# Folding the width axis twice on VectorE, width transforms in groups of 160, and small TensorE tiles placed side by side

## The chip, the core and the metric

One core of one Trainium2 chip runs the whole program. The metric is device time of one execution in microseconds (us); the number for a kernel is the median of its runs. Engines are named as in the profile: PE is TensorE (PEld its weight loads), DVE is VectorE, ACT is ScalarE, POOL is GpSimd, SP issues the DMAs.

## What is computed

```python
def reference(A_x, A_w_r, A_w_i, B_x, B_w1, B_b1, B_w2, B_b2):
    # A: y = irfft2(rfft2(x over rows S=2048 and width D=640) * (w_r + 1j*w_i))
    # B: h = gelu_tanh(x @ w1 + b1), 640 -> 1536; y = h @ w2 + b2, 1536 -> 640
    x = A_x                                    # (1, 2048, 640), bf16
    xn = _layernorm(x, axis=-1)
    return x + _A_ref(xn, A_w_r, A_w_i) + _B_ref(xn, B_w1, B_b1, B_w2, B_b2)
```

## The kernel before

The 2048 rows are held as 16 chunks `c` of 128 partitions. Every transform is a product with a constant table that is loaded from HBM. The program is a list of operations with priorities and guessed durations; a planner (`Sched`) fixes, when the program is built, the order on each engine, which of ACT or DVE makes a copy, and which of the eight PSUM slots a result takes. Each engine then runs its list strictly in order and waits on semaphores. The stages:

- **Ring stage** (per chunk): DVE makes the layernorm statistics of two chunks at a time (L528 to L534; the power -1/2 is on POOL, L532, `rstd`), normalizes (L547), and folds the width once (L562): the sum and the difference of the row and its mirror image, 320 columns each. PE transposes the normalized chunk (L554, five matmuls with `ident`) for the dense branch, and multiplies the folded chunk by `gtab` (five matmuls of 128 columns), a first step of the row transform. DVE or ACT copies both from PSUM (`xnT`, `XW`).
- **First dense layer**: 48 groups of five matmuls of 512 columns (`xnT`, `W`), each followed by one gelu on ACT (`gT`, L583) that adds the bias column `b1col`. The planner gives these groups to PE where it has nothing more urgent. The bias column is made by a small matmul and a DVE copy (L512, L514), both with priority 50 while the ring has about 100.
- **Spectral stage** (eight pairs of 128-row groups `q`): six matmuls of 320 columns with `etab` per group (the width transform), a copy (`Xb`), four of 322 with `mtab`, a copy (`Y`), two DVE multiplications by the filter (`T`, L622) and five DVE additions (`Z`, L632, L636) per pair, ten matmuls of 128 with `ntab`, a copy (`XV`).
- **Final stage** (per chunk): six matmuls of 320 with `getab` (the inverse width transform), a copy (`Wf`), then 24 matmuls of 320 of the second dense layer (`gT`, `XW` which by then holds W2) and four of 320 with `htab` into the same PSUM. Two of the four exist only because the width is still folded. POOL adds x and the bias b2 beforehand (L688, `b2bc`), DVE adds that to PSUM (`ost`, L704), and a DMA writes the chunk. Groups of the first dense layer that are left over stand between.

Nearly all matmuls are recorded under one helper line, L450, all copies under L457 (ACT) and L458 (DVE), so groups are told apart by the names of their tiles. SP issues the loads in the order written: x, `ident`, W1, `gtab`, `etab`, `mtab`, 24 pieces of the filter, `ntab`, `getab`, `htab`, `b2bc`, W2.

Of the kernel before, what the change touches and what calls it, by code (L numbers as in the profile page):

```python
# [288 lines left out]
def _tables():  # L289
    pi = np.pi  # L290
    T = {}
    s1 = np.arange(128)
    G = np.zeros((128, 16, 128))
    H = np.zeros((128, 16, 128))
    for s2 in range(16):
        for q in range(16):
            for i in range(4):
                m1 = 16 * i + q
                ang = 2 * pi * ((m1 * (16 * s1 + s2)) % 2048) / 2048
                G[:, s2, q * 8 + i] = np.cos(ang)  # L300
                G[:, s2, q * 8 + 4 + i] = -np.sin(ang) if m1 else np.cos(pi * s1)
                H[q * 8 + i, s2] = np.cos(ang)
                H[q * 8 + 4 + i, s2] = np.sin(ang) if m1 else np.cos(pi * s1)
    T["G"], T["H"] = G, np.stack([H, -H], axis=2)
    th = 2 * pi * ((np.arange(321)[:, None] * (2 * np.arange(320)[None, :] + 1)) % 1280) / 1280
    ck = np.where((np.arange(321) == 0) | (np.arange(321) == 320), 1.0, 2.0)[:, None] / (S * D)
    Ec, Es = np.cos(th)[:320].T, -np.sin(th)[1:].T
    GEc, GEs = (ck * np.cos(th))[:320], (-ck * np.sin(th))[1:]

    def five(a, b):  # L310
        z = np.zeros((64, 320))
        return np.concatenate([a[0:128], a[128:256], np.concatenate([a[256:320], z]), np.concatenate([z, b[0:64]]),
                               b[64:192], b[192:320]], axis=1)
    T["E"] = five(Ec, Es)

    T["GE"] = five(GEc, np.concatenate([GEs[256:320], GEs[0:256]]))
    M = np.zeros((2, 4, 128, 128))
    N = np.zeros((2, 2, 128, 128))
    for sp in range(2):
        for i in range(4):  # L320
            for m2 in range(16):
                p = 16 * i + m2
                s2 = np.arange(16)
                r, u = s2 * 8 + i, s2 * 8 + 4 + i
                a1 = 2 * pi * ((m2 * s2) % 16) / 16
                c, s = np.cos(a1), np.sin(a1)
                rr, ir, ri, ii = M[sp]
                NA, NB = N[sp]
                if sp and i == 0:
                    pq = 64 + m2  # L330
                    a2 = 2 * pi * ((s2 * (2 * m2 + 1)) % 32) / 32
                    c2, t2 = np.cos(a2), np.sin(a2)
                    rr[r, p], ri[r, p], ir[r, p], ii[r, p] = c, s, -s, c
                    rr[u, pq], ri[u, pq], ir[u, pq], ii[u, pq] = c2, t2, -t2, c2
                    NA[p, r], NB[p, r], NA[pq, u], NB[pq, u] = c, s, c2, t2
                    continue
                pq = 64 + 16 * ((4 if sp else 3) - i) + 15 - m2
                rr[r, p], rr[u, p], ir[r, p], ir[u, p] = c, s, -s, c
                ri[r, p], ri[u, p], ii[r, p], ii[u, p] = s, -c, c, s
                rr[r, pq], rr[u, pq], ir[r, pq], ir[u, pq] = c, s, s, -c  # L340
                ri[r, pq], ri[u, pq], ii[r, pq], ii[u, pq] = -s, c, c, s
                NA[p, r], NA[pq, r], NB[p, r], NB[pq, r] = c, c, s, -s
                NA[p, u], NA[pq, u], NB[p, u], NB[pq, u] = -s, -s, c, -c
    T["M"] = M.transpose(2, 0, 1, 3)
    T["N"] = np.stack([N[:, 0], N[:, 1], -N[:, 1]], axis=1).transpose(2, 0, 1, 3)
    T["I"] = np.eye(128)
    return T
# [392 lines left out]
```

## Time and profile before

| | |
|---|---|
| median of 3 runs | 197.65 us (197.29 to 197.73) |
| profiled execution, its own time | 198.18 us |
| its span, first to last instruction | 196.4 us |
| PE busy | 172.5 us (88%), 1265 matmuls |
| DVE, ACT, POOL busy | 88.3, 75.1, 28.3 us |
| mean granted TensorE clock | 0.974 of full speed |
| DMA | 17.84 MB |

Busy times are sums over the whole span; PE's includes stretches at the lower clock. A matmul's recorded duration includes the time that it takes to leave the array, so that the records of neighbours overlap: the pace of a run of matmuls is read from the start of one group to the start of the next.

### The profile page before, as it was taken

To read this page: it belongs to the slowest core of one execution; us is meant where nothing else is said; L and a number is where in the kernel's file an instruction comes from. 1 tells how busy PE (TensorE), PEld (TensorE's weight loads), DVE (VectorE), ACT (ScalarE), POOL (GpSimd) and SP (SyncE) were. 2 spreads that over 40 slices of the span, in tenths; PEclk is the share of its full clock that TensorE was granted. 3 is DMA by queue.
4 is the path that set the end of the run, shared out by engine and by line. 5 is a ranking of instruction groups with operands and counts; after the bars stand their busy time and mean duration, and the time that the engine had idled before them with its cause. 6 is when DMAs were issued, how large, how long until landed. Compare 5 with 4: busy or idle time off the path is not lost.

```text
span 196.4 us, 3073 instructions
## 1 busy us (share of the span) xinstructions
PE 172.5 (88%) x1265; PEld 113.7 (58%) x1265; DVE 88.3 (45%) x221; ACT 75.1 (38%) x110; POOL 28.3 (14%) x32
## 2 busy tenths in 40 slices
PE   0149760899999999999999999999999999999993
PEld 0135420566567777875677777775457775436772
DVE  0999899869619899967111111111001111001211
ACT  2004500845477679885711111114651113660100
POOL 1111112200000000000823222222002222000200
PEclk9999996589999999999999999999999999999999
DMA  6999999990000000039422222222000201000111
GB/s 179 378 394 301 120 120 132 139 355 13 3 0 0 3 3 0 3 76 376 135 82 71 69 67 68 77 80 79 0 3 33 67 33 37 0 0 0 37 54 48
DMA packets 14374, 17.84 MB, mean 91 GB/s; under 512 B 1304, under 2 KB 13208, under 8 KB 14232
## 3 DMA queue, kind: packets, MB, share of 16 engines
q1 hardware_dynamic: 14360, 17.65, 35.8%
q8 instruction: 10, 0.16, 0.4%
q14 instruction: 4, 0.03, 0.1%
HBM read 15.02 MB, written 2.62 MB: 90 GB/s over the span
## 4 chain that ended last, share of the span: by engine, by line
PE 85%; DVE 11%; DMA 2%; ACT 0%; issue 0%
PE ps L450 82%; DVE stats L528 5%; PE ps L554 4%; DMA XV<-in_A_x_dram 2%; DVE T L547 1%; DVE T L562 1%; DVE mv L530 1%; DVE xnT L458 1%; DVE ost L704 0%; DVE XW L458 0%; ACT gT L583 0%; DVE nmr L534 0%; DVE ve L531 0%; DVE b1col L514 0%
## 5 line engine op out<-in xcount | busy, mean ns | idle before, releaser
L450 PE MATMUL ps<-xnT,W 128*128 128x512 bf16 x240 | 56.9, 388 | 0.0
L450 PE MATMUL ps<-XW,gT 128*128 128x320 bf16 x384 | 54.8, 299 | 0.8 <-ACT gT L583 0.8
L704 DVE TENSOR_TENSOR ost<-ps,Wf 128x640 bf16<-128x640 f32 x16 | 13.2, 824 | 87.0 <-PE ps L450 87.0
L450 PEld LDWEIGHTS ps<-XW,gT 128*128 128x128 bf16 x384 | 37.5, 98 | 15.9 <-ACT gT L583 1.5
L583 ACT ACTIVATE gT<-ps,b1col 128x512 bf16<-128x512 f32 x48 | 32.3, 689 | 30.6 <-PE ps L450 20.1
L688 POOL TENSOR_TENSOR Wf<-Wf,b2bc 128x640 f32<-128x640 bf16 x16 | 22.2, 1394 | 125.1 <-DVE ost L704 67.1
L450 PEld LDWEIGHTS ps<-xnT,W 128*128 128x128 bf16 x240 | 23.5, 100 | 25.1 <-issue 1.7
L457 ACT ACTIVATE Wf<-ps 128x640 bf16<-128x640 f32 x16 | 11.2, 703 | 52.2 <-PE ps L450 51.9
L554 PE MATMUL ps<-ident,T 128*128 128x128 bf16 x80 | 8.8, 277 | 12.5 <-DVE b1col L514 7.2
L528 DVE BATCH_NORM_STATS2 stats<-XV 128x6 f32<-128x320 bf16 x32 | 13.7, 467 | 4.9 <-DMA XV<-in_A_x_dram 4.9
L450 PE MATMUL ps<-getab,XV 128*128 128x320 bf16 x96 | 15.3, 299 | 0.0
L554 PEld LDWEIGHTS ps<-ident,T 128*128 128x128 bf16 x80 | 6.8, 126 | 14.7 <-DVE b1col L514 7.7
L450 PE MATMUL ps<-etab,XW 128*128 128x320 bf16 x96 | 14.7, 299 | 0.0
L622 DVE TENSOR_TENSOR T<-Y,Wf 128x1288 bf16<-128x1288 bf16 x16 | 12.5, 823 | 0.6 <-ACT Y L457 0.5
L457 ACT ACTIVATE Xb<-ps 128x640 bf16<-128x640 f32 x15 | 10.6, 706 | 3.3 <-PE ps L450 2.5
L450 PEld LDWEIGHTS ps<-etab,XW 128*128 128x128 bf16 x96 | 9.4, 97 | 3.9
L450 PEld LDWEIGHTS ps<-getab,XV 128*128 128x128 bf16 x96 | 9.4, 98 | 3.8 <-ACT XV L457 0.2
L450 PE MATMUL ps<-Wf,htab 128*128 128x320 bf16 x64 | 11.3, 299 | 0.0
L457 ACT ACTIVATE XW<-ps 128x640 bf16<-128x640 f32 x6 | 4.1, 700 | 17.9 <-PE ps L450 17.9
L450 PE MATMUL ps<-Xb,mtab 128*128 128x322 bf16 x64 | 10.4, 300 | 0.0
L450 PE MATMUL ps<-ntab,Z 128*128 128x128 bf16 x160 | 10.2, 219 | 0.0
L450 PEld LDWEIGHTS ps<-ntab,Z 128*128 128x128 bf16 x160 | 9.6, 98 | 0.9
(33 smaller groups left out, 107.7 us busy)
## 6 DMA issues: line engine op xcount, KB each, us to landing
XV<-in_A_x_dram SPq DMA_DIRECT2D x4, 640.0 KB, 8.0
Wf<-in_A_x_dram SPq DMA_DIRECT2D x16, 160.0 KB, 2.2
out_dram<-ost SPq DMA_DIRECT2D x16, 160.0 KB, 1.8
W<-in_B_w_dram SPq DMA_DIRECT2D x3, 640.0 KB, 7.7
XW<-in_B_w_dram SPq DMA_DIRECT2D x1, 1920.0 KB, 8.0
htab<-c_H SPq DMA_DIRECT2D x1, 1024.0 KB, 11.5
Wf<-in_A_w_r_dram SPq DMA_DIRECT2D x4, 160.5 KB, 13.5
Wf<-in_A_w_i_dram SPq DMA_DIRECT2D x4, 160.5 KB, 12.3
```

Source lines behind the costliest of these rows:

```text
L450: ins = e.matmul(o_, lhsT=lw, rhs=rh, start=st, stop=sp_)
L457: return e.activation(dst(), src(), ACT.Copy)
L458: return e.tensor_copy(dst(), src())
L528: K.op([("dve", 0.4)], pr, lambda e, _, c=c, h=h: e.bn_stats(stats[:, c, 6 * h:6 * h + 6], view(XV, c * D + H2 * h, [[1, H2]])), reads=[B_ ...
L530: K.op([("dve", 0.12)], pr, lambda e, _, c=c: e.bn_aggr(mv[:, c, :], stats[:, c, :]), reads=[B_st[c - a]], writes=[B_mv])
L547: norm_ops.append(K.op([("dve", 0.32)], pr, lambda e, _, c=c, xnv=xnv: e.tensor_scalar(out=xnv(0, [[1, D]]), in0=view(XV, c * D, [[1, D]]) ...
L554: ins = e.transpose(ps(tps.slot, 0, 512).bitcast(BF)[:, 128 * j:128 * j + 128], xnv(128 * j, [[1, 128]]), ident[:])
L562: K.op([("dve", dve_us(H2, 2))], pr - 0.2, lambda e, _, k=k, op=op, xnv=xnv, xfv=xfv: e.tensor_tensor(out=xfv(H2 * k, [[1, H2]]), in0=xnv( ...
L583: K.op([("act", act_us(512, 1))], pr + 50, lambda e, _, q4=q4, fc=fc, hps=hps: e.activation(gT[:, fc, 512 * q4:512 * q4 + 512], ps(hps.slo ...
L622: filt_ops.append(K.op([("dve", dve_us(4 * KP, 2))], pr, lambda e, _, k=k, Y=Y, TB=TB, pair=pair: e.tensor_tensor(out=view(TT, TB.slot * 8 ...
L688: K.op([("pool", pool_us(640))], 50, lambda e, _, xr=xr, xo=xo: e.tensor_tensor(out=xov(xo), in0=view(Wf, XR + xr.slot * D, [[1, D]]), in1 ...
L704: K.op([("dve", dve_us(640))], 95, lambda e, _, xo=xo, os_=os_, fps=fps: e.tensor_tensor(out=ost[:, os_.slot, :].rearrange("p (h n) -> p h ...
```

## The change

The row is folded a second time: after the first fold DVE adds and subtracts the two halves of each 320 columns again, which leaves four groups of 160. The width transform and its inverse then work in groups of 160 on a table of 800 columns (`etab`, `getab`) in place of 1920. As 160 is 128 and 32, each product has a full part and a rest of 32; the four rests are stored together as a fifth block of 128, and a helper, `five`, issues them as matmuls that use 32 of the array's rows. Where the rests are on the output side (`gtab`, `ntab`), four matmuls with 32 weight columns write to partitions 0, 32, 64 and 96 of one PSUM bank. The products with `mtab` become eight matmuls of 64 rows by 64 columns of weights, four to a position of the array. On the way out DVE unfolds two chunks at once: two operations from 160 to 320, two from 320 to 640, so that only two matmuls with `htab` per chunk are left, and `htab` has half its columns.

Beside that: the bias column's priority is 200; `Z` is made in two operations per pair in place of five; x and its sum with b2 have buffers of their own (`xr`, `xo`), so that their loads wait for nothing; every wait of an engine for an earlier operation of its own (but on PE) is now a semaphore wait; and the durations by which the planner decides are other numbers.

```diff
@@ durations for the planner @@
 def mm_us(n):
-    return max(n / 2400.0 + 0.003, 0.061)
+    return max(n / 2400.0 + 0.003, 0.0265)
...
-LAT = {"pe": 0.25, "dve": 0.12, "act": 0.15, "pool": 0.15}
+LAT = {"pe": 0.2, "dve": 0.12, "act": 0.15, "pool": 0.1}
@@ Sched.sync @@
                     if o.eng == "pe":
                         continue
-                    raw = any(d in b.writers for b in o.reads)
-                    if not raw:
-                        continue
                 need.append(d)
@@ tables @@
-        etab = sb("etab", [128, 1920])
-        mtab = sb("mtab", [128, 8, 128])
+        etab = sb("etab", [128, 800])
+        mtab = sb("mtab", [128, 2, 2, 2, 64])
-        getab = sb("getab", [128, 1920])
-        htab = sb("htab", [128, 32, 128])
+        getab = sb("getab", [128, 800])
+        htab = sb("htab", [128, 16, 128])
@@ bias column @@
-        K.op([("pe", 0.1)], 50, lambda e, _: e.matmul(ps(B_b1ps.slot, 0, NFC), ...
+        K.op([("pe", 0.1)], 200, lambda e, _: e.matmul(ps(B_b1ps.slot, 0, NFC), ...
-        K.op([("dve", 0.2)], 50, lambda e, _: e.tensor_copy(b1col[:], ...
+        K.op([("dve", 0.08)], 200, lambda e, _: e.tensor_copy(b1col[:], ...
@@ second fold, product with gtab @@
+            for k, op in enumerate((ALU.add, ALU.subtract)):
+                K.op([("dve", dve_us(H2, 2))], pr - 0.2, lambda e, _, k=k, op=op, x1v=x1v, xfv=xfv: e.tensor_tensor(
+                    out=xfv(Q4 * k, [[H2, 2], [1, Q4]]), in0=x1v(0, [[H2, 2], [1, Q4]]), in1=x1v(H2 - 1, [[H2, 2], [-1, Q4]]), op=op),
+                    reads=[x1], writes=[xf])
-                (ps(aps.slot + j // 4, 128 * (j % 4), 128 * (j % 4) + 128), xfv(128 * j, [[1, 128]]), gtab[:, c, :], True, True) for j in range(5)]),
+                (ps(aps.slot, 128 * g, 128 * g + 128), xfv(Q4 * g, [[1, 128]]), gtab[:, c, :], True, True) for g in range(4)] + [
+                (ps(aps.slot + 1, 0, 128)[32 * g:32 * g + 32], xfv(Q4 * g + 128, [[1, 32]]), gtab[:, c, :], True, True) for g in range(4)]),
@@ width transform, forward (etab) and back (getab) @@
+        def five(o_, main, rem, tab, v):
+            lst = []
+            for n, order in enumerate(((0, 1), (1, 0))):
+                for k, part in enumerate(order):
+                    for g in (2 * v, 2 * v + 1):
+                        if part == 0:
+                            lst.append((o_(g - 2 * v, n), main(g, n), tab[:, Q4 * g:Q4 * g + Q4], k == 0, k == 1))
+                        else:
+                            lst.append((o_(g - 2 * v, n), rem(g, n), tab[32 * g:32 * g + 32, 4 * Q4:5 * Q4], k == 0, k == 1))
+            return lst
-                    (ps(bps.slot + (n > 2), 0, H2), Xa[:, j, q, :], etab[:, H2 * n:H2 * n + H2], n in (0, 3), n in (2, 5))
-                    for n, j in enumerate((0, 1, 2, 2, 3, 4))]), reads=B_xa + [B_e], writes=[bps], gate=[cps_ops.get(q - 2)]))
+                    lambda b, n: ps(bps.slot + b, Q4 * n, Q4 * n + Q4), lambda g, n: Xa[:, g, 2 * pair + n, :],
+                    lambda g, n: Xa[32 * g:32 * g + 32, 4, 2 * pair + n, :], etab, v)), reads=B_xa + [B_e], writes=[bps], gate=cps_ops.get(pair - 2, [])))
@@ product with mtab @@
-                    (ps(cps.slot + r, 0, KP), mtab[:, (4 if q == 0 else 0) + 2 * v + r, :], xb4[:, xb.slot, KP * v:KP * v + KP], v == 0, v == 1)
-                    for r in range(2) for v in range(2)]), ...
+                    (ps(cps.slot + hi, 0, KP)[64 * qq:64 * qq + 64], mtab[64 * hi:64 * hi + 64, 1 if pair == qq == 0 else 0, v, r, :],
+                     xb4[64 * hi:64 * hi + 64, xb.slot, (2 * qq + v) * KP:(2 * qq + v + 1) * KP], v == 0, v == 1)
+                    for v in range(2) for hi in range(2) for qq in range(2)]), ...
@@ product with ntab: eight of 128 columns, then eight rests @@
+                            lst.append((ps(dps.slot, 128 * g, 128 * g + 128), z(r, k0, 128), rh, n == 0, n == 1))
...
+                            lst.append((ps(dps.slot + 1, 0, 128)[32 * g:32 * g + 32], z(r, k0 + 256, 32), rh, n == 0, n == 1))
@@ unfolds (DVE, per two chunks), x and b2, product with htab @@
+                K.op([("dve", dve_us(D, 2))], pr + 2, lambda e, _, k=k, op=op, yo=yo, y2=y2: e.tensor_tensor(
...
+                K.op([("dve", dve_us(D, 2))], pr + 3, lambda e, _, k=k, op=op, y2=y2, yf=yf: e.tensor_tensor(
...
+                K.op([("sp", 0.06)], 0, lambda e, _, c=c, xr=xr: e.dma_start(xrt[:, xr.slot, :], xv[:, c, :]), writes=[xr], nbytes=163840)
...
-                lst.append((ps(fps.slot, 0, H2), htab[:, 2 * c, :], ye, False, False))
-                lst.append((ps(fps.slot, 0, H2), htab[:, 2 * c, :], yod, False, True))
-                lst.append((ps(fps.slot + 1, 0, H2), htab[:, 2 * c, :], yer, False, False))
-                lst.append((ps(fps.slot + 1, 0, H2), htab[:, 2 * c + 1, :], yor, False, True))
+                    for h in range(2):
+                        lst.append((ps(fps.slot + h, 0, H2), htab[:, c, :], view(Wf, YF + yf.slot * 2 * D + D * n + H2 * h, [[1, H2]]), False, True))
```

What the planner makes of it shows in three places. First DVE: before, the copy of the bias column (`b1col`) stands behind the statistics of the last chunks but two of the ring, 70 rows down the list (`ve`, `mv`, `nmr` are the small layernorm operations).

```order
L530 BN_AGGR mv<-stats 128x2
L528 BN_STATS stats<-XV 128x6 x2
L534 SCALAR_TENSOR_TENSOR nmr<-mv,rstd 128x2
L530 BN_AGGR mv<-stats 128x2
L514 COPY b1col<-ps 128x12
L531 TENSOR_SCALAR ve<-mv 128x2
```

Now it stands at the list's start, and the second folds (L575) follow the first (L572) chunk by chunk.

```order
L534 BN_STATS stats<-XV 128x6
L520 COPY b1col<-ps 128x12
L537 TENSOR_SCALAR ve<-mv 128x2
L536 BN_AGGR mv<-stats 128x2
L534 BN_STATS stats<-XV 128x6 x2
L540 SCALAR_TENSOR_TENSOR nmr<-mv,rstd 128x2
L536 BN_AGGR mv<-stats 128x2
L553 TENSOR_SCALAR T<-XV,rstd,nmr 128x640 x2
L572 TENSOR_TENSOR T<-T 128x320 x2
L463 COPY xnT<-ps 128x5x128
L575 TENSOR_TENSOR T<-T 128x2x160 x2
```

The bias copy moved ahead of the first normalization. Second POOL, whose list is short: before, the eight `rstd` of the layernorm come first and the sums of x and b2 after them.

```order
L463 MEMSET mhalf 128x16
L464 MEMSET Xb 128x3x3
L465 MEMSET Xb 128x3
L466 MEMSET Wf 128x32
L532 ISA
L532 TENSOR_TENSOR rstd<-ve,mhalf 128x2 x8
L688 TENSOR_TENSOR Wf<-Wf,b2bc 128x640 x16
```

After:

```order
L468 MEMSET mhalf 128x16
L469 MEMSET Xb 128x4x3
L470 MEMSET Xb 128x4
L471 MEMSET Wf 128x32
L538 ISA
L538 TENSOR_TENSOR rstd<-ve,mhalf 128x2 x6
L713 TENSOR_TENSOR xo<-xr,b2bc 128x640 x3
L538 TENSOR_TENSOR rstd<-ve,mhalf 128x2 x2
L713 TENSOR_TENSOR xo<-xr,b2bc 128x640 x13
```

Three sums of x and b2 now stand in front of the last two `rstd`, those of chunks 12 to 15. Third PE in the spectral stage, where `etab`, `mtab` and `ntab` name the three products and `xnT,W` the first dense layer: before,

```order
L450 MATMUL ps<-Xb,mtab 128x322 x8
L450 MATMUL ps<-etab,XW 128x320 x12
L450 MATMUL ps<-xnT,W 128x512 x5
L450 MATMUL ps<-Xb,mtab 128x322 x8
L450 MATMUL ps<-etab,XW 128x320 x6
L450 MATMUL ps<-ntab,Z 128x128 x20
L450 MATMUL ps<-Xb,mtab 128x322 x4
L450 MATMUL ps<-etab,XW 128x320 x12
```

and after, where 64x322 and 32x128 are the small tiles:

```order
L455 MATMUL ps<-Xb,mtab 64x322 x32
L455 MATMUL ps<-etab,XW 128x160 x32
L455 MATMUL ps<-xnT,W 128x512 x5
L455 MATMUL ps<-Xb,mtab 64x322 x16
L455 MATMUL ps<-etab,XW 128x160 x8
L455 MATMUL ps<-ntab,Z 128x128 x8
L455 MATMUL ps<-ntab,Z 32x128 x8
L455 MATMUL ps<-ntab,Z 128x128 x8
L455 MATMUL ps<-ntab,Z 32x128 x8
```

The order of the three products is much as it was; the pieces are more and smaller, and full matmuls and small ones alternate. In the whole list, groups of the first dense layer stand before, within and behind the spectral stage as 17, 9 and 22 of the 48 before, and as 26, 7 and 15 after.

## Rows read from the trace of the kernel before

**Rows 1.** From the page: chain that ended last, and GB/s in 40 slices

```profile
PE 85%; DVE 11%; DMA 2%; ACT 0%; issue 0%
GB/s 179 378 394 301 120 120 132 139 355 13 3 0 0 3 3 0 3 76 376 135 82 71 69 67 68 77 80 79 0 3 33 67 33 37 0 0 0 37 54 48
```

**Rows 2.** Busy time by stage: stretch, length, engines with counts, granted clock, DMA

```profile
core 0: us, PE busy (x) PEld busy (x) DVE busy (x) ACT busy (x) POOL busy (x), PEclk, DMA share, GB/s
...
9.10:27.90 18.80, 14.96 (x105) 9.10 (x105) 17.80 (x61) 4.69 (x6) 2.25 (x4) 1.00 1.13 248
27.90:35.20 7.30, 0.07 (x2) 0.03 (x2) 7.30 (x30) 0.05 (x1) 1.89 (x3) 0.71 1.22 129
35.20:41.70 6.50, 6.49 (x43) 4.48 (x44) 3.96 (x11) 4.79 (x8) 0.69 (x1) 0.54 1.15 209
...
54.03:94.53 40.50, 40.50 (x367) 28.91 (x366) 31.65 (x67) 30.51 (x46) 0.52 (x1) 1.00 0.21 66
94.53:193.30 98.77, 97.97 (x655) 63.78 (x653) 12.37 (x15) 27.05 (x39) 21.71 (x16) 1.00 0.15 46
193.30:196.40 3.10, 0.00 (x0) 0.00 (x0) 0.82 (x1) 0.00 (x0) 0.00 (x0) 1.00 0.16 56
```

**Rows 3.** Timeline of PE and ACT: start, length, instruction, [idle before, releaser]

```profile
35.17 3.08 PE L554 MATMUL ps<-ident,T 128*128 128x128 bf16 x25 [7.23 <-DVE b1col L514]
...
35.15 4.15 ACT L583 ACTIVATE gT<-ps,b1col 128x512 bf16<-128x512 f32 x7 [10.44 <-DVE b1col L514]
```

**Rows 4.** Timeline of PE in the spectral stage, a stretch without a gap

```profile
59.47 1.24 PE L450 MATMUL ps<-xnT,W 128*128 128x512 bf16 x5
60.55 1.26 PE L450 MATMUL ps<-Xb,mtab 128*128 128x322 bf16 x8
61.66 0.98 PE L450 MATMUL ps<-etab,XW 128*128 128x320 bf16 x6
62.47 1.28 PE L450 MATMUL ps<-ntab,Z 128*128 128x128 bf16 x20
63.59 0.71 PE L450 MATMUL ps<-Xb,mtab 128*128 128x322 bf16 x4
```

**Rows 5.** Timeline of PE in the final stage, one chunk

```profile
101.59 3.42 PE L450 MATMUL ps<-XW,gT 128*128 128x320 bf16 x24
104.85 0.71 PE L450 MATMUL ps<-Wf,htab 128*128 128x320 bf16 x4
```

**Rows 6.** From the page, costliest groups: busy us, mean ns of one

```profile
L450 PE MATMUL ps<-ntab,Z 128*128 128x128 bf16 x160 | 10.2, 219 | 0.0
```

**Rows 7.** Timeline of DVE in the ring stage: normalization, folds, copies from PSUM

```profile
28.73 0.75 DVE L547 TENSOR_SCALAR T<-XV,rstd,nmr 128x640 bf16<-128x640 bf16 x2
29.40 1.02 DVE L562 TENSOR_TENSOR T<-T 128x320 bf16<-128x320 bf16 x4
...
44.49 1.54 DVE L458 CAST XW<-ps 128x640 bf16<-128x640 f32 x2
```

**Rows 8.** Timeline of POOL: the seventh power of the layernorm, the first three sums

```profile
33.99 0.69 POOL L532 TENSOR_TENSOR rstd<-ve,mhalf 128x2 f32<-128x2 f32 x1 [2.72 <-DVE ve L531]
...
94.01 4.09 POOL L688 TENSOR_TENSOR Wf<-Wf,b2bc 128x640 f32<-128x640 bf16 x3 [57.96 <-DMA Wf<-in_A_x_dram]
```

**Rows 9.** Issue of the load of b2 (SP's timeline) and its landing (the tile's view)

```profile
34.25 0.45 SPq L445 DMA_DIRECT2D b2bc<-in_B_b_dram  x1
...
DMA to landing us min/median/max: 11.4/11.4/11.4
```

**Rows 10.** Timelines of DVE and ACT in the spectral stage: filter, additions, copies

```profile
68.93 1.56 DVE L622 TENSOR_TENSOR T<-Y,Wf 128x1288 bf16<-128x1288 bf16 x2
70.52 0.63 DVE L636 TENSOR_TENSOR Z<-T 128x640 bf16<-128x640 bf16 x2
...
63.27 1.30 ACT L457 ACTIVATE XV<-ps 128x640 bf16<-128x640 f32 x2
```

More of the change, by code (lines that the diff above doesn't have):

```diff
@@ L16 @@
 H2 = 320
+Q4 = 160
 KP = 322
@@ L27, with mm_us, dve_us, act_us @@
+def mm_us(n):
+    return max(n / 2400.0 + 0.003, 0.0265)
+def dve_us(n, rate=1.0):
+    return 0.066 + n / 960.0 / rate
+def act_us(n, ptr=0):
+    return 0.052 + n / 1200.0 + 0.092 * ptr
+def pool_us(n):
+    return 0.075 + n / 500.0
 class Buf:
@@ L72 @@
 class Op:
-    __slots__ = ("engs", "eng", "prio", "reads", "writes", "after", "emit", "seq", "start", "end", "ready",
-                 "nbytes", "gate", "name", "deps", "inc", "count", "sem", "known", "waits", "done")
-LAT = {"pe": 0.25, "dve": 0.12, "act": 0.15, "pool": 0.15}
+    pass
+LAT = {"pe": 0.2, "dve": 0.12, "act": 0.15, "pool": 0.1}
 class Sched:
@@ L286, in emit @@
         block.tensor(run("pe"))
[L289 to L347, printed above, removed]
@@ L639, in bass_parallel_sum__spectral_gfnet__dense_activation_gelu__prompt_kernel @@
-            for qq in range(2):
-                q = 2 * pair + qq
-                dps = Buf(f"dps{q}", psum, 2)
-                def ipc(q=q, qq=qq, Z=Z, dps=dps):
-                    n0 = 3 if q == 0 else 0
+            filt_ops += t_ops[pair]
+            for r, op in enumerate((ALU.subtract, ALU.add)):
+                K.op([("dve", dve_us(2 * KP, 2))], pr, lambda e, _, TB=TB, Z=Z, r=r, op=op: e.tensor_tensor(
+                    out=view(Zb, Z.slot * 4 * KP + r * KP, [[2 * KP, 2], [1, KP]]), in0=tv(TB, 0, r), in1=tv(TB, 1, r), op=op), reads=[TB], writes=[Z])
@@ L645, in ipc, with z @@
+            for hi in range(2):
+                dps = Buf(f"dps{pair}_{hi}", psum, 2)
+                def ipc(pair=pair, hi=hi, Z=Z, dps=dps):
+                    n0 = 3 if pair == hi == 0 else 0
                     NA, NB, NN = ntab[:, n0, :], ntab[:, n0 + 1, :], ntab[:, n0 + 2, :]
-                    def z(off):
-                        return bass.AP(tensor=Zb, offset=Z.slot * 1540 + qq * 770 + off, ap=[[3080, 128], [1, 128]])
+                    def z(r, k0, n):
+                        return view(Zb, Z.slot * 4 * KP + (2 * hi + r) * KP + k0, [[2, n]])
@@ L661, in ipc @@
[L661 to L664 removed]
+                    for g, k0 in enumerate((0, 1, 1, 2)):
+                        for n, (r, rh) in enumerate(((0, NA), (1, NN)) if g < 2 else ((1, NA), (0, NB))):
+                            lst.append((ps(dps.slot, 128 * g, 128 * g + 128), z(r, k0, 128), rh, n == 0, n == 1))
@@ new lines, in ipc @@
+                    for n in range(2):
+                        for g, k0 in enumerate((0, 1, 1, 2)):
+                            r, rh = (((0, NA), (1, NN)) if g < 2 else ((1, NA), (0, NB)))[n]
+                            lst.append((ps(dps.slot + 1, 0, 128)[32 * g:32 * g + 32], z(r, k0 + 256, 32), rh, n == 0, n == 1))
+                    return lst
+                K.op([("pe", 8 * mm_us(128) + 8 * mm_us(32))], 90 - pair / 5, mms(ipc), reads=[Z, B_n], writes=[dps])
+                K.op([("act", act_us(640)), ("dve", dve_us(640))], 90 - pair / 5,
+                     copy(lambda pair=pair, hi=hi: view(XV, 8 * (2 * pair + hi), [[2048, 5], [128, 16], [1, 8]]),
```

278 lines of the change are left out of this document (161 added, 117 removed).

## The prediction

> **What bounds the kernel now.** I read the chain that ended last first: 85% of it is PE, 11% DVE [rows 1]. Cut by stage [rows 2], that splits cleanly. From 54.0 us to the end PE is never free: 40.50 of 40.50 us in the spectral stage, 97.97 of 98.77 in the final one, at full clock. There a microsecond taken off PE is a microsecond of time, unless something else takes its place; ACT and DVE are busy for 30.5 and 31.7 of the 40.5 us, so that they are next. Ahead of 54 us DVE sets the pace: it is busy for 17.80 of 18.80 us and then 7.30 of 7.30, while PE stands still from 27.9 to 35.2. What ends that gap is the bias copy, `b1col` [rows 3]: until it runs, ACT has waited 10.44 us with seven gelus, their PSUM slots are held, and PE has waited 7.23 us. The stretch behind it runs at a granted clock of 0.54, the lower of the two levels (1.2 GHz): of its 6.5 us some 3.0 are lost. So two things can pay: less PE work after 54 us, and dense groups moved into the ring stage, where PE has room.
>
> **Prices.** From start to start at full clock [rows 4]: a dense group 1.08 us; eight of `mtab` 1.11, so 0.139 each; six of `etab` 0.81, so 0.135; twenty of `ntab` 1.12, so 0.056. The 24 of the second dense layer take 3.26 us [rows 5], 0.136 each. Between 128 and 320 columns a matmul of 160 is put at 0.069.
>
> Two prices no row shows. **Small tiles side by side:** whether four that use different parts of the array take the time of one (lower end) or of four (upper end). I take the lower end: a small tile streams as many columns as a full one, and the parts don't share rows and columns both. **Changing between full and small tiles:** nothing at best, since shapes of 512, 320 and 128 follow each other in rows 4 without a gap; at worst the array empties first, which is the record's length less its pace, 219 - 56 = 163 ns [rows 6, 4]. I take 40 ns, near the rows without a gap. There are 32 changes with `gtab`, 32 with `etab`, 10 with `mtab` (its sets stand in runs), 32 with `ntab`, 32 with `getab`.
>
> The Trainium skill, TensorEngine Tiling (Array Packing), Key Properties, says that a change of tiling mode, not of tile alone, drains the engine; no row here shows one, and the first rival below is what that would do. Its page TensorE: Matmul & The Clock Gate, Part 3 (packing small matmuls), gives 3.07 times for four row tiles where four would be ideal; by that the sets would cost some 0.3 more, an estimate of 3.5 us on top of my sum. Neither enters it.
>
> **The change, part by part.**
>
> *PE work.* `five`: four full ones 0.276, four rests in twos 0.138, two changes 0.08: 0.49 against 0.81. Sixteen with `etab` save 5.1 us, sixteen with `getab` 5.1. `mtab`: 32 sets of four at 0.139 and ten changes, 4.9 against 8.9: 4.0 saved. `ntab`: eight at 0.056, two sets of rests, two changes, 0.64 against 0.56: 1.3 more. `gtab`: 0.36 against 0.28: 1.3 more, in the ring. `htab`: two of four go, 32 x 0.136 = 4.4 saved. PE's sum falls by 16.0 us.
>
> *Ring stage.* The bias copy at the list's head lets ACT start its gelus as soon as a dense group is done, so the wait of 7.23 us and its low clock go [rows 3, 2]. What is late next: DVE, and then POOL. DVE: the seventh `rstd` ran at 33.99 [rows 8]; the list in front of its user gets 24 second folds and four more first folds (28 x 0.235 = 6.6 us, from the 1.02 for four less the overlap of the last, [rows 7]), two more copies of `XW` (1.5 us by the 1.54 for two, [rows 7]) and 0.4 for the bias, less one transposed copy of about that: 34.7 + 8.1, DVE is there at about 43 us. If the second fold with its strides ran at half the rate, it would be 5 us later still. POOL: three sums now stand ahead of that `rstd`, and they need `b2bc`. It landed at 34.25 + 11.4 = 45.65 [rows 9]; the tables in front of it shrink by 1.23 MB, 3.2 us at the 380 GB/s of the early slices [rows 1]; x's first chunk follows it. So the sums begin at 42.9, take 4.09 and the power 0.69 [rows 8]: DVE gets it at 47.7 and stands for 4 to 5 us. Behind its waiting `nmr` in DVE's list are four normalizations, eight first folds, eight second ones and the last copies, 7.9 us: 55.6. PE waits for the normalized chunk until 48.4 and has four transposes (0.28), four `gtab` (0.36) and six dense groups left, 9.1 us: 57.5. A gap of about 4 us may lower its clock as the 7.23 did; half of that loss is 1.5. **The spectral stage begins at 59** (55 without POOL's stall, 62 with the whole loss of clock), 5 us later than before, but with 26 dense groups done in place of 17, worth 9.7 us.
>
> *Spectral stage.* PE: 7.8 + 4.9 + 10.2 and seven dense groups (7.6) = 30.5 us. ACT: 40 copies at 0.60 to 0.65 [rows 10] and seven gelus at 0.58 (4.15 for seven, less the overlap of the last, [rows 3]) = 28 to 30. DVE: per pair the filter 1.59, two `Z` at about 0.45 (one of 640 and one of 128 start to end 0.63, [rows 10]), and eight copies of 0.77 in all = 26. So three engines are nearly level, and their lists are in strict order; a pair needs about 6 us from its first matmul to its last copy, of which most of the last pair's shows. I take **35 us** (31.5 to 40) against 40.5.
>
> *Final stage.* Fifteen dense groups 16.2, sixteen `five` 7.8, sixteen chunks at 3.26 + 0.27 = 56.5: **80.7 us** with the end of the last matmul, against 98.8. The unfolds, 32 of 640 columns, cost DVE 0.4 to 0.75 each (between a fold's rate and a copy's), under 3 us per 8 us of two chunks, in a stage where it was busy for 12 of 99 us [rows 2]; they are planned one pair of chunks ahead, so PE's 8 us of other work hides them. Uncovered, the four would cost 2 to 3 us once. The new waits for own earlier operations cost DVE under 0.1 us where the operation in front is the one waited for; nothing I count.
>
> *Sum.* 59 + 35 + 80.7 + 3.1 (the end, as in rows 2) = 177.8 us of span. The profiled execution took 198.18 us for 196.4 of span, and the median is 0.5 below it: 177.8 + 1.8 - 0.5 = **179.1 us**.
>
> **The rivals.**
> - *Each change of tile empties the array* (0.163 each). In the spectral stage 74 changes x 0.123 = 9.1 us: PE's sum 39.6, the stage 41.5; in the final one 32 x 0.123 = 3.9. Together 10.4 more: 189.5. For it: the matmul's 163 ns beyond its pace, which something must wait for where the array is set anew. Against it: no gap between any two shapes so far. (The skill's rule on draining is this one; that it is a full drain no run here shows.) Chance 0.11.
> - *Small tiles run one after another.* `mtab` 96 x 0.139 = 13.3 us more, `ntab` 96 x 0.056 = 5.4, `etab` and `getab` 2.2 each. PE's sum in the spectral stage is then 51.4, the stage 53.4; with 2.2 at the end and 0.7 in the ring that is 21.3 more: 200.4, **slower than before**. It decides from seven eighths of that price. `mtab` carries it: there the two tiles of the same 64 rows stream different columns, which no row shows to be possible. Chance 0.09.
> - *Copies bind in the spectral stage.* With PE's work at 30 us, ACT's order or DVE's becomes the bound, PE waits in each pair: 40 us, 184. For it: in rows 2 both already fill three quarters of the stage. Chance 0.14.
> - *POOL's sums don't hold DVE* (the load of b2 lands earlier, or DVE comes later): 55 in place of 59, 175. Chance 0.07.
>
> **How the numbers follow.** The forecast has 0.59, 173 to 186. The low end of all is 55 + 31.5 + 79.5 + 3.1 + 1.3 = 170.4; the emptied array reaches 190, with a part of the other price 194. Range 170 to 194, leaving out little but the serial case. A measurement of this kernel can tell 0.2% from no change. Slower needs most of the serial price, or half of it with the emptied array: 0.10. Within 0.2%: 0.02. Faster: 0.88.
>
> **What would show it.** PE's long gap at 28 to 35 us gone; a POOL sum waiting for `b2bc` at 43 us and DVE's `nmr` waiting for POOL for 4 to 5 us; `five` at 0.49 from start to start, a set of four `mtab` at 0.14 and not 0.28 or 0.56; dense groups after small tiles without a gap; 59, 94 and 175 as the stages' ends; PE no longer full in the spectral stage. Wrong would be: small tiles at multiples of these prices, or ACT waited for throughout the spectral stage.

## The result, and the profile after

Over four runs of each on one chip the changed kernel takes 191.7 us (190.8 to 194.19) against 197.69 (197.29 to 197.84): a ratio of 0.9685, with a 95% interval of 0.9646 to 0.9724. One of its four runs, 194.19, counts as slow; the ratio is that of the others, whose median is 191.5. The change makes the kernel faster by 6.0 us where 18.6 were forecast. The profiled execution took 190.8 us for a span of 189.2.

The page of the changed kernel, its chain and its GB/s slices, answers to [rows 1]:

```profile
PE 163.8 (87%) x1505; PEld 99.7 (53%) x1505; DVE 99.7 (53%) x248; ACT 84.5 (45%) x123; POOL 28.5 (15%) x32
...
GB/s 176 378 388 275 98 110 99 106 96 287 101 83 0 3 0 0 7 3 0 280 139 3 0 13 95 69 107 69 69 71 71 69 35 52 21 0 0 35 69 38
...
PE 67%; SPq 14%; DMA 10%; DVE 3%; POOL 3%; ACT 1%; issue 1%
```

PE's share of the chain fell from 85% to 67%, and a quarter of it is now DMA and the queue that issues it. The stretches say where; the columns are those of [rows 2]:

```profile
9.25:44.40 35.15, 32.31 (x252) 18.02 (x253) 32.85 (x115) 22.48 (x33) 3.63 (x5) 1.00 1.18 167
44.40:54.64 10.24, 1.21 (x7) 0.37 (x5) 0.70 (x4) 1.37 (x2) 4.74 (x4) 0.69 0.55 184
54.64:66.06 11.42, 11.42 (x82) 6.26 (x83) 7.74 (x25) 6.01 (x9) 0.75 (x1) 0.83 0.03 9
66.06:103.14 37.08, 36.71 (x554) 21.80 (x554) 25.23 (x40) 33.16 (x48) 0.00 (x0) 1.00 0.18 55
103.14:186.50 83.36, 81.96 (x615) 53.21 (x613) 28.64 (x49) 20.17 (x30) 18.13 (x13) 1.00 0.15 48
```

The gap of 7.3 us at 28 to 35 is gone: up to 44.4 us PE is busy for 32.31 of 35.15. In its place stands a hole of 10.24 us in which PE works for 1.21, DVE for 0.70 and POOL for 4.74. The timelines of POOL, DVE and PE (columns as in [rows 3]) name it:

```profile
49.16 4.08 POOL L713 TENSOR_TENSOR xo<-xr,b2bc 128x640 f32<-128x640 bf16 x3 [12.88 <-DMA xr<-in_A_x_dram]
53.20 0.70 POOL L538 TENSOR_TENSOR rstd<-ve,mhalf 128x2 f32<-128x2 f32 x1
...
43.38 0.83 DVE L534 BATCH_NORM_STATS2 stats<-XV 128x6 f32<-128x320 bf16 x2
53.94 0.16 DVE L540 SCALAR_TENSOR_TENSOR nmr<-mv,rstd 128x2 f32<-128x2 f32 x1 [9.73 <-POOL rstd L538]
...
54.64 1.25 PE L560 MATMUL ps<-ident,T 128*128 128x128 bf16 x10 [9.03 <-DVE T L553]
55.68 2.34 PE L455 MATMUL ps<-xnT,W 128*128 128x512 bf16 x5
```

POOL's three sums stand in its list ahead of the power that DVE needs. They wait 12.88 us for a load; DVE, which was done at 44.2, stands for 9.73 us; PE for 9.03; and five matmuls of a dense group then take 2.34 us where five at full clock take 1.24, since the granted clock is back at its lower level (1.2 GHz). Then PE is full to the end.

The final stage begins and ends with these rows of PE's timeline; the dense group at 102.05 is the first of the fifteen that the forecast counts into the final stage, and the last matmul ends at 185.9:

```profile
102.05 1.25 PE L455 MATMUL ps<-xnT,W 128*128 128x512 bf16 x5
...
185.44 0.43 PE L455 MATMUL ps<-Wf,htab 128*128 128x320 bf16 x2
```

Forecast and measured: the spectral stage begins at 59 / 66.06, the final stage at 94 / 102.05, the last matmul ends at 175 / 185.9. So of the 11.4 us of span that were missed, 7.1 lie in the ring stage, 1.0 in the spectral one (36.0 for 35), 3.1 in the final one (83.8 for 80.7) and 0.2 behind the last matmul. The stretches above and below, which end at the first `getab`, have one dense group more in the spectral stage and one less in the final one.

### The profile page after: what moved, and what is told of

It is laid out like the page before. It is cut to its first block, busy times and chain, and to the rows that moved or that the text cites. A ratio compares the mean times of both kernels' runs of the same rounds, so it can differ in the third digit from the quotient of the medians.

```text
span 189.2 us, 3594 instructions
## 1 busy us (share of the span) xinstructions
PE 163.8 (87%) x1505; PEld 99.7 (53%) x1505; DVE 99.7 (53%) x248; ACT 84.5 (45%) x123; POOL 28.5 (15%) x32
## 4 chain that ended last, share of the span: by engine, by line
PE 67%; SPq 14%; DMA 10%; DVE 3%; POOL 3%; ACT 1%; issue 1%
PE ps L455 66%; SPq L450 14%; DMA xr<-in_A_x_dram 7%; DMA XV<-in_A_x_dram 2%; POOL xo L713 2%; DVE stats L534 1%; PE ps L560 1%; DVE Y L463 1%; POOL rstd L538 1%; DVE ost L725 0%; ACT XV L462 0%; ACT gT L598 0%; ACT Y L462 0%; DVE T L553 0%; DVE mv L536 0%
## 5 line engine op out<-in xcount | busy, mean ns | idle before, releaser
L713 POOL TENSOR_TENSOR xo<-xr,b2bc 128x640 f32<-128x640 bf16 x16 | 22.2, 1393 | 114.7 <-DVE ost L725 101.8
L725 DVE TENSOR_TENSOR ost<-ps,xo 128x640 bf16<-128x640 f32 x16 | 13.2, 824 | 47.2 <-PE ps L455 47.2
L455 PE MATMUL ps<-ntab,Z 128*128 128x128 bf16 (+1 forms) x256 | 12.8, 223 | 0.2 <-ACT Y L462 0.2
L462 ACT ACTIVATE XV<-ps 128x640 bf16<-128x640 f32 x16 | 11.2, 709 | 1.1 <-PE ps L455 0.4
L455 PEld LDWEIGHTS ps<-ntab,Z 128*128 128x128 bf16 (+1 forms) x256 | 9.5, 97 | 3.9 <-issue 0.8
L700 DVE TENSOR_TENSOR Wf<-Wf 128x640 bf16<-128x640 bf16 x16 | 8.0, 537 | 5.8 <-ACT Wf L462 5.8
L455 PE MATMUL ps<-getab,XV 128*128 128x160 bf16 (+1 forms) x128 | 11.0, 234 | 0.0
L455 PE MATMUL ps<-etab,XW 128*128 128x160 bf16 (+1 forms) x128 | 10.9, 234 | 0.1
L538 POOL TENSOR_TENSOR rstd<-ve,mhalf 128x2 f32<-128x2 f32 x8 | 5.8, 722 | 33.8 <-DVE ve L537 33.8
L455 PEld LDWEIGHTS ps<-gtab,T 128*128 128x128 bf16 (+1 forms) x128 | 7.0, 101 | 5.7 <-issue 1.1
```

Source lines behind the costliest of these rows:

```text
L455: ins = e.matmul(o_, lhsT=lw, rhs=rh, start=st, stop=sp_)
L462: return e.activation(dst(), src(), ACT.Copy)
L538: K.op([("pool", 0.6)], pr, lambda e, _, a=a, b=b: e.tensor_tensor(out=rstd[:, a:b], in0=ve[:, a:b], in1=mhalf[:, a:b], op=ALU.pow), reads ...
L700: K.op([("dve", dve_us(D, 2))], pr + 2, lambda e, _, k=k, op=op, yo=yo, y2=y2: e.tensor_tensor(out=view(Wf, Y2 + y2.slot * 2 * D + (H2 - 1 ...
L713: K.op([("pool", pool_us(640))], 50, lambda e, _, xr=xr, xo=xo: e.tensor_tensor(out=xot[:, xo.slot, :], in0=xrt[:, xr.slot, :], in1=b2bc[: ...
L725: K.op([("dve", dve_us(640))], 95, lambda e, _, xo=xo, os_=os_, fps=fps: e.tensor_tensor(out=ost[:, os_.slot, :].rearrange("p (h n) -> p h ...
```

## The experiments

**The order on POOL, and the bias column alone.** The first kernel puts POOL's powers ahead of its sums and moves nothing else on any engine; the second is the kernel before with the bias copy early and no other edit; the planner then places the dense groups anew.

```
 e1_powers_first, in the changed kernel:
-            K.op([("pool", 0.6)], pr, ... pow ...)
+            pow_ops.append(K.op([("pool", 0.6)], pr, ... pow ...))
...
-  op=ALU.add), reads=[xr, B_b2b], writes=[xo])
+  op=ALU.add), reads=[xr, B_b2b], writes=[xo], gate=pow_ops)

 e7_bias_alone, in the kernel before (matmul and copy of b1col):
-        K.op([("pe", 0.1)], 50, ...
+        K.op([("pe", 0.1)], 200, ...
-        K.op([("dve", 0.2)], 50, ...
+        K.op([("dve", 0.2)], 200, ...
```

> The changed kernel with one thing undone: the planner may place POOL's sums of x and b2 only behind all eight powers of the layernorm. The lists of PE, DVE, ACT and SP stay as they are. Theory: of the 11.4 us by which the changed kernel's span missed the forecast, the wait of DVE for POOL (9.73 us) and the low clock behind PE's gap of 9.03 us are the larger part. Then nmr of chunks 12 and 13 runs at 44.6 in place of 53.94, the gap of PE goes, the spectral stage begins at 55 to 56 in place of 66.06, and the time falls by 10 to 11 us, to about 181. Rival: the gap was cover for something else that is late (the filter's load, the copies of the spectral stage); then PE waits there instead, and the time falls by 3 to 5 us only, to about 187.

> The kernel before with one part of the change alone: the bias column's matmul and copy have priority 200. Theory: most of what the change gained is this part. PE's gap of 7.23 us and the low clock behind it (3.0 us lost) go, dense groups move into the ring stage, and the time falls by 6 to 9 us, to 189 to 192, as far as the whole change. Rival: the ring stage is set by DVE, and PE's freed time is not used; 2 to 3 us, to 195.

e1: **180.49 us**, a ratio to before of 0.9079 (0.9043 to 0.9115). POOL's timeline in e1:

```profile
44.46 0.69 POOL L538 TENSOR_TENSOR rstd<-ve,mhalf 128x2 f32<-128x2 f32 x1 [7.08 <-DVE ve L537]
48.37 0.75 POOL L538 TENSOR_TENSOR rstd<-ve,mhalf 128x2 f32<-128x2 f32 x1 [3.22 <-DVE ve L537]
53.30 4.22 POOL L713 TENSOR_TENSOR xo<-xr,b2bc 128x640 f32<-128x640 bf16 x3 [4.18 <-DMA xr<-in_A_x_dram]
```

And e1's ring stage in two stretches (columns as in [rows 2]):

```profile
9.25:44.00 34.75, 30.90 (x245) 17.38 (x246) 32.55 (x115) 21.52 (x32) 3.91 (x6) 1.00 1.19 158
44.00:56.13 12.13, 12.13 (x96) 6.48 (x94) 9.75 (x33) 8.16 (x13) 4.27 (x5) 1.00 0.82 162
```

The sums now begin even later, at 53.30, and nobody waits for them; the hole is gone, the clock stays at 1.00, and the spectral stage begins at 56.1. From 191.7 to 180.49 the stall was worth 11.2 us (14.4 between two single runs on one chip, h2 and h3 below), more than its 9.03 us of PE, since the low clock behind it goes too.

e7: **187.74 us**, 0.9466 (0.9416 to 0.9516). The bias column alone is worth 10.3 us, more than the whole change. By [rows 3] and [rows 2] it had to give 7.23 us of gap and 3.0 of low clock, 10.2; the 6 to 9 that were written before the run were too little.

**The folds without the bias.** The kernel of e1 with the bias column back at its late place:

```
-        K.op([("pe", 0.1)], 200, ...   # matmul and copy of b1col
+        K.op([("pe", 0.1)], 50, ...
```

> The kernel of e1_powers_first (180.49 us) with the bias column back at its late place (about 35 us). Two questions. What the early bias column is worth in the folded kernel: alone on the kernel before it was worth 10.3 us; if it is worth as much here, 190.8 us; if DVE's and POOL's work of the ring stage covers the gap, 183 or less. And what slows the filter's load, which ran at 120 to 145 GB/s in the kernel before and at 87 to 114 in those with the early bias column: if it is the work of PE, ACT and DVE beside it, it returns to 120 or more while they stand still; if it is the order of the tables in the queue, it stays near 90 to 100.

It takes 196.59 us, 0.9927 (0.9892 to 0.9963): both expectations were too fast. With the bias late, folds, unfolds, small tiles and the smaller edits together are worth 1.4 us, with it early 187.74 - 180.49 = 7.3. Two of its stretches show why (columns as in [rows 2]):

```profile
25.00:37.00 12.00, 1.49 (x9) 0.62 (x8) 11.87 (x48) 0.31 (x2) 2.10 (x4) 0.65 1.23 91
...
98.80:192.50 93.70, 92.79 (x665) 58.11 (x663) 28.15 (x49) 27.04 (x40) 18.13 (x13) 1.00 0.14 43
```

DVE sets the pace of the ring stage [rows 2] and gets the added folds there; from 25 to 37 us PE works for 1.49 of 12 while DVE is busy for 11.87. The ten dense groups that it can't do (665 matmuls in the last stage in place of the 615 of the changed kernel) come back at the end. With the bias early, PE does them while DVE folds.

**The rate of the filter's load.** Why were the sums so late? The load of b2 is issued at 34.19 us, as before [rows 9], but lands 14.5 us later in place of 11.4, and x's first chunk behind it (rows as in [rows 9]):

```profile
34.19 0.82 SPq L450 DMA_DIRECT2D b2bc<-in_B_b_dram  x1
...
DMA to landing us min/median/max: 14.5/14.5/14.5
```

What stands ahead of both is the filter. The kernel before loaded it at 120 to 139 GB/s [rows 1], the changed one at 96 to 110. One idea was the direction: the changed kernel reads the mirrored rows backwards.

```
 e2_filter_ascending: mirrored pieces read ascending, written descending
+            if step < 0:
+                off, row = off + 2 * KP * (n - 1), row - (n - 1)
-  ap=[[WP, 16], [2 * KP, n], [1, 321]]), ... ap=[[128 * 321, 16], [step * 321, n], [1, 321]])
+  ap=[[WP, 16], [step * 2 * KP, n], [1, 321]]), ... ap=[[128 * 321, 16], [321, n], [1, 321]])
```

> The changed kernel, where the pieces of the filter that are read from HBM with descending rows are read with ascending rows and written with a descending step, as the kernel before did; nothing else differs, and every engine's list is the same. Theory: the descending reads are why the filter's load ran at 95 to 114 GB/s in place of 120 to 137, so that the load of b2 landed at 48.7 and not at 42.5. Then b2 lands some 4 us earlier, POOL's sums begin at 45 in place of 49.16, and the time falls by 4 us, to 187.5. Rival: the rate has another cause (how the pieces lie over partitions, or other traffic at the same time); then the load and the time stay: 191.7.

193.99 us, 0.9793 (0.9767 to 0.9819), 91 GB/s from 20 to 38 us: the direction isn't it. Nor does the rate come back when PE stands: in g5 (above), which has the new pieces, it was 91 GB/s. So the three kernels were run once more on one chip, and then the kernel before with the new pieces alone.

> The kernel before, unchanged, looked at once more beside the changed one on one chip, for the rate at which the filter is loaded. Theory A (the rate belongs to the kernel): 120 to 135 GB/s between 20 and 38 us, as in its first profile, and 198 us. Theory B (the rate differs from execution to execution or from chip to chip): anywhere from 85 to 135.

> The changed kernel, unchanged, on the same chip. Theory A (the rate of the filter's load belongs to the kernel): 101 to 107 GB/s as in its first profile, sums of POOL from 49 us, 191 us. Theory B (it differs by execution or chip): another rate, and the sums and the time follow it: at 90 GB/s the sums begin some 5 us later, at 52 to 54, and the time is about 194 to 196.

> The kernel of e1_powers_first, unchanged, on the same chip as the other two. Theory A: 87 to 98 GB/s as in its first profile. Theory B: a rate near that of the other two kernels on this chip. The time is 180.5 us in either case, since nothing waits for the load there.

```
 h4_new_filter_loads, in the kernel before: 12 issues for each plane become 9
-  for h in range(4): for half in range(2): ... part(0, 16, 1, 0) or part(0, 1, 1, 0), part(1, 15, -1, 15)
+  for qq in range(2): for lo in range(2): ... load_w(wsrc, p0, ...), load_w(wsrc, p0 + 32, ...)
```

> The kernel before with one edit: the filter is loaded by the changed kernel's 18 issues (pieces of 16 partitions in the new order of rows, part of them read backwards) in place of its own 24; everything else is as before, so that the filter's rows lie in other places than its multiplication assumes. Theory A (the new pieces are what slows the filter's load): 87 to 107 GB/s between 20 and 44 us, in place of 112 to 130. Theory B (what slows it is the work of the engines beside it or the tables ahead of it): 112 to 130, as in the kernel before. The time is near 198 us by both, since nothing there waits for the load.

The stretch from 26 to 32 us of h1 (columns as in [rows 2]):

```profile
26.00:32.00 6.00, 1.47 (x7) 0.49 (x5) 6.00 (x24) 0.00 (x0) 1.38 (x2) 0.84 1.23 122
```

of h2:

```profile
26.00:32.00 6.00, 6.00 (x55) 3.30 (x52) 6.00 (x22) 4.69 (x8) 0.00 (x0) 1.00 1.23 94
```

and of h4:

```profile
26.00:32.00 6.00, 1.56 (x8) 0.49 (x5) 6.00 (x24) 0.00 (x0) 1.38 (x2) 0.85 1.22 89
```

h1 took 197.53 us, h2 194.87, h3 180.52, h4 197.62. The kernel before keeps its rate (112 to 130 GB/s). The changed kernel had 92 to 96 here and 102 to 107 in its first profile, so its rate does scatter, and its sums and its time go with it: from 52.8 us, and 194.87. h4, with engines as busy as in h1, had 89: the new pieces alone can bring the rate down, by more than the tenth by which it scatters (one run each, on two chips). In h3 the load is as slow (87 to 98) and costs nothing.

But the new pieces aren't needed for it either. e7 has the old ones, and a PE that is never free; its rate was 104 to 113 GB/s, and its b2 landed at 51.0, later than the 48.7 of the changed kernel (the rows of b2, and the stretch as for h1):

```profile
36.86 0.55 SPq L445 DMA_DIRECT2D b2bc<-in_B_b_dram  x1
...
DMA to landing us min/median/max: 14.1/14.1/14.1
...
26.00:32.00 6.00, 6.00 (x48) 3.52 (x47) 6.00 (x21) 3.94 (x6) 0.04 (x1) 1.00 1.22 110
```

So the early bias column with its busier engines, or the scatter, may have slowed the changed kernel's load (104 GB/s from 20 to 38 us, e7's 107) as well as the pieces; no run here has the old pieces in the changed kernel. Two more runs asked which property of the pieces:

```
 h5_filter_order: the same 18 pieces; neighbours 64 partitions apart, not 32
-  for qq in range(2): for lo in range(2): straight piece, mirrored piece
+  for lo in range(2): for qq in range(2): straight piece
+  for lo in range(2): for qq in range(2): mirrored piece
 h6_filter_order_asc: h5 with the edit of e2
```

> The changed kernel (190.8 us profiled, sums of POOL from 49.2) with one edit: the same 18 pieces of the filter, issued in another order, so that pieces that follow each other go to partitions 64 apart, as in the kernel before, and not 32 apart; engines' lists are the same. Theory A (the distance of neighbouring pieces sets the rate): 112 GB/s or more between 20 and 38 us, the sums from 46 us, 187 us. Theory B (it is the pieces themselves): 86 to 107 GB/s, the sums from 49 to 53, 190 to 195 us.

> As h5_filter_order, and the mirrored pieces are read ascending and written descending (the direction that the kernel before uses). With this only the number of split pieces differs from its way. Theory A (order and direction together set the rate): 112 GB/s or more and 187 us. Theory B (neither does): 86 to 107 GB/s and 190 to 195 us.

The single runs of the changed kernel and its variants, worked out from their stretches and timelines:

| kernel | GB/s, 20 to 38 us | sums begin | spectral begins | profiled, us |
|---|---|---|---|---|
| h5_filter_order | 115 | 46.5 | 64.4 | 189.26 |
| h6_filter_order_asc | 102 | 48.1 | 65.3 | 189.99 |
| changed, first profile | 104 | 49.2 | 66.1 | 190.80 |
| e2_filter_ascending | 91 | 51.4 | 68.4 | 193.23 |
| h2_after_again | 94 | 52.8 | 70.1 | 194.87 |

The spectral stage begins 17 to 18 us behind the sums each time. h5 has the highest rate of any kernel with the new pieces (113 to 117 GB/s) and the earliest sums, though 189.26 us and not the 187 that was expected; h6, with the same order, is at 99 to 104 and within the scatter of the changed kernel. So it isn't shown that the order of pieces sets the rate, and why the rate differs, between kernels and between two runs of one, stays open.

**The price of a change of tile.** The first kernel adds two changes to each `five`: both columns take full tile, then rest, where the second had begun with its rest.

```
 e6_more_changes
-            for n, order in enumerate(((0, 1), (1, 0))):
+            for n, order in enumerate(((0, 1), (0, 1))):
```

> The changed kernel, where in each group of eight matmuls of the width transform (etab, getab) the order full, full, rest, rest, rest, rest, full, full becomes full, full, rest, rest, full, full, rest, rest. The same matmuls on the same data, with two more changes between full and small tiles per group. Theory A (a change between tile shapes costs about 105 ns, the rests themselves run side by side): the pace of a group goes from 0.625 to 0.83 us, 3.3 us more in the final stage and up to as much in the spectral stage: 195 to 198. Theory B (changes are nearly free, the small tiles run one after another): the pace stays at 0.625 and the time at 191.7.

200.47 us, 1.0106 (1.0057 to 1.0156). PE's timeline in the final stage, two `five` and what follows, in the changed kernel:

```profile
115.03 1.41 PE L455 MATMUL ps<-getab,XV 128*128 128x160 bf16 x16
116.28 3.42 PE L455 MATMUL ps<-XW,gT 128*128 128x320 bf16 x24
```

and in e6:

```profile
122.44 1.73 PE L455 MATMUL ps<-getab,XV 128*128 128x160 bf16 x16
124.10 2.08 PE L455 MATMUL ps<-XW,gT 128*128 128x320 bf16 x14
```

From start to start 1.25 us become 1.66: 0.41 for four more changes, 103 ns each. The 195 to 198 us that were expected were too few: of the 9.6 us between the two profiled runs, 3.4 lie in the spectral and 3.4 in the final stage, as priced, and 2.8 ahead of them, since the sums began at 51.98 in place of 49.16. The same price falls out of the changed kernel: a `five` at 0.625 less six at 0.069 leaves 0.21 for two.

The next kernels take changes out of e1. One multiplies the rests as full matmuls against a table padded with zeros, the other lets the second inverse group of a pair begin with its rests, the third does both.

```
 g1_full_rests: tables of 1280 columns, the 32 rows of a group at their place, zeros elsewhere
-  rem(g, n), tab[32 * g:32 * g + 32, 4 * Q4:5 * Q4], ...
+  rem(g, n), tab[:, (4 + g) * Q4:(5 + g) * Q4], ...
-  lambda g, n: V[32 * g:32 * g + 32, 4, 2 * cp + n, :]      (Xa likewise)
+  lambda g, n: V[:, 4, 2 * cp + n, :]
 g2_rests_by_tile
+                    full, lst = lst, []      (between full matmuls and rests)
-                    return lst
+                    return lst + full if hi else full + lst
```

> The kernel of e1_powers_first (180.49 us), with one edit: in the width transforms the rest of 32 columns of the width is multiplied as a matmul over all 128 partitions against a table that holds the 32 rows of its group and zeros elsewhere (1280 table columns in place of 800), so that no change of tile is left in the groups with etab and getab; mtab, ntab and gtab keep their small tiles. Theory A (a change of tile costs about 105 ns, the tiles of a pair run side by side): a five becomes eight full matmuls at 0.069 = 0.55 us in place of 0.625, 0.073 less each; sixteen with getab give 1.2 us in the final stage and sixteen with etab 1.2 in the spectral one: 178.2 us. Theory B (the spectral stage is set by ACT's copies): only the 1.2 of the final stage, 179.3. Rival (small tiles are cheap and the surplus of a five lies elsewhere, in the strided reading of the columns): no gain or a loss, 180.5 to 182.

> The kernel of e1_powers_first (180.49 us), with one edit: of the two inverse groups of a pair with ntab, the second issues its rests ahead of its full matmuls, so that the rests of both stand together: two changes of tile fewer wherever the two follow each other. Theory A (105 ns per change): the two take about 1.35 us in place of 1.56, over eight pairs 1.7 us less in the spectral stage if PE sets its pace: 178.8 us. Theory B (ACT's copies set the spectral stage): the two are shorter but the stage is not, 180.5 us.

> The kernel of e1_powers_first (180.49 us) with the edits of g1_full_rests and g2_rests_by_tile together. Theory A: 180.49 - 2.4 - 1.7 = 176.4 us. Theory B (ACT sets the spectral stage): 179.3 us.

g1: **177.81 us**, 0.9004 (0.8949 to 0.9059), where 178.2 was expected. g2: 180.33, 0.9038 (0.8976 to 0.91); two of its four runs took 178.9, where 178.8 was expected, two 181.7 and 183.85. g3: **176.45**, 0.892 (0.8878 to 0.8961), where 176.4 was expected. The medians of g2 and e1 can't be told apart; the stage can. The spectral stretch (columns as in [rows 2]) of e1:

```profile
56.13:93.20 37.07, 36.70 (x554) 21.78 (x553) 25.24 (x40) 33.19 (x48) 1.40 (x2) 1.00 0.21 67
```

of g1:

```profile
55.10:91.00 35.90, 35.53 (x554) 24.82 (x553) 25.17 (x40) 32.81 (x48) 1.96 (x2) 1.00 0.23 71
```

of g2:

```profile
55.70:91.30 35.60, 35.21 (x553) 21.65 (x552) 25.17 (x40) 32.66 (x48) 0.00 (x0) 1.00 0.20 62
```

and of g3:

```profile
56.20:90.70 34.50, 34.12 (x554) 24.71 (x554) 25.16 (x40) 32.03 (x48) 0.95 (x1) 1.00 0.22 69
```

Two `five` of g1, from PE's timeline in the final stage:

```profile
110.60 1.27 PE L460 MATMUL ps<-getab,XV 128*128 128x160 bf16 x16
111.70 3.42 PE L460 MATMUL ps<-XW,gT 128*128 128x320 bf16 x24
```

Eight full matmuls take 0.55 us (1.10 for two `five`), less than four full, two pairs of small ones and two changes at 0.625: here zeros are cheaper than tiles. The stage shrinks by 1.2, 1.5 and 2.6 us, as PE's work does, so PE sets its pace and not ACT, which is busy for 32.0 of 34.5 in g3.

## Why the prediction missed its number

**Right.** The direction, and every mechanism of the ring stage: the gap behind `b1col` goes; POOL's sums hold the power, DVE's `nmr` waits for POOL, PE for DVE, and the clock falls behind it. Small tiles run side by side: 16 of `mtab` take 0.68 us from start to start, where four sets at the price of one and the change behind them make 0.66, and one after another they would take 2.2 (the second row is what follows). Two of four `htab` go (0.27 for 0.54). The unfolds cost 0.49 to 0.54 each, within the bounds, and no PE wait follows from them. The new waits for own operations show in no engine's waits.

```profile
74.83 0.74 PE L455 MATMUL ps<-Xb,mtab 64*64 64x322 bf16 x16
75.51 0.80 PE L455 MATMUL ps<-etab,XW 128*128 128x160 bf16 x8
```

**Wrong, the start of the sums (42.9 forecast, 49.16 measured).** The step took 3.2 us off the landing of b2 because less table stood in front of it, and let the rest of the queue run as before. That was the failed term: the filter in front of b2 loaded at about 104 GB/s in place of 120 to 139, and b2 landed at 48.7, 3 us later than before and not 3 earlier. The new pieces alone can slow the load so far (h4), and a kernel with the early bias column and the old pieces was as slow (e7); which of them did it here stays open. DVE was done at 44.2 (43 forecast) and stood for 9.73 us where 4 to 5 were written. The sum's 59 became 66: 6.3 of the 7.1 us by this alone. e1 shows what the stall is worth.

**Wrong in size, the change of tile (40 ns forecast, 105 measured, 163 as upper bound).** With 40 a `five` was 0.49 and is 0.625, an `ntab` group 0.64 and is 0.78 (four in 3.12, the rows below), a `gtab` group 0.36 and is 0.49. In the final stage 16 x 0.135 = 2.2 of the 3.1 us missed; a wait of 0.8 for a gelu is most of the rest. In the spectral one 74 x 0.065 = 4.8 us of PE work, 35.3 in place of 30.5, so that PE and not the lists of ACT and DVE became the bound: 36.0 in place of 35. That the forecast came so near there was luck: it gave 4.5 us to those lists, which cost next to nothing, and missed as much in the changes.

```profile
90.08 3.18 PE L455 MATMUL ps<-ntab,Z 128*128 128x128 bf16 x64
93.20 1.35 PE L455 MATMUL ps<-Xb,mtab 64*64 64x322 bf16 x32
```

The row that decided for 40, no gap between 512, 320 and 128 columns [rows 4], changes the columns that stream and never the tile; it said nothing on this. The Trainium skill, TensorEngine Tiling (Array Packing), Key Properties, says that a change of tiling mode drains the engine; the runs agree that a change costs, at about two thirds of the record's 163 ns. The estimate of 3.5 us for sets that fall short of their ideal (the Trainium skill, TensorE: Matmul & The Clock Gate, Part 3) isn't seen: six at 0.069, ten at 0.056 and eight at 0.139 with changes at 105 ns leave nothing.

**The rivals.** The emptied array: a change does cost, though 105 ns and not 163; its 189.5 is near the result by accident, since most of what was missed lay in the ring. Serial tiles: not so. Copies bind: ACT came to 33.2 of 37.1 us, above the 28 to 30 forecast, mostly since a copy of `Xb` with its new stride takes 0.911 us where it took 0.706 (13 of them, 2.7 us; the groups below); but the stage still went with PE (g1 to g3). Without POOL's stall, e1 gives 56.1 for the start of the spectral stage, near the 55 of that rival, and 180.5 us for its 175, with the true price of changes.

ACT's copies of `Xb`, from the page's costliest groups (busy us, mean ns of one, idle before), in the kernel before:

```profile
L457 ACT ACTIVATE Xb<-ps 128x640 bf16<-128x640 f32 x15 | 10.6, 706 | 3.3 <-PE ps L450 2.5
```

and in the changed one, with the copies of `Wf`, which read PSUM in the same order but write without the stride:

```profile
L462 ACT ACTIVATE Xb<-ps 128x640 bf16<-128x640 f32 x13 | 10.5, 911 | 0.5 <-PE ps L455 0.4
L462 ACT ACTIVATE Wf<-ps 128x640 bf16<-128x640 f32 x15 | 9.9, 703 | 35.5 <-PE ps L455 35.5
```

**The attribution.** The forecast spoke of PE's 16 us as the main term. By the runs the early bias is 10.3 us alone; folds and tiles add 7.3 once POOL's list is mended, and nearly nothing (1.4) with the bias late. As built, the stall took 11.2 back.

The best of the kernels is g3, at 176.45 us: early bias, powers first, zeros in place of small tiles in the width transforms, and rests side by side in the inverse ones.

## What to carry to other kernels

Before a saving on the engine that sets a later stage is counted, look at the in-order list of the engine that feeds the stage, and put nothing that waits for a late load ahead of what others wait for: one gate was worth 11 us here. Small tiles pay by the run of equal ones; where four of them cost two changes, padding with zeros can be cheaper. A change that moves a load's bytes to new rows and partitions can change its rate too (122 GB/s became 89 between h1 and h4), so don't take a landing time from the old rate as given: put what others wait for where a late landing can't hold it.
